# Exponentials by bits on VectorE: which engine writes the bits, when V's weights are loaded, and where the last branches stand

## The chip, the cores and the metric

The kernel runs on one core of one Trainium2 chip. A core has TensorE (matrix products, called PE in the profile; its weight loads PEld), VectorE (DVE), ScalarE (ACT), GpSimd (POOL) and SyncE (SP, which here issues nearly all DMAs). The metric is the time of one execution on the device in microseconds; lower is better. Inputs and output are bf16.

## The reference

Two branches work on the same input x of 2048 rows and 1024 columns, and a gate mixes them.

```
x = A_x
g = _sigmoid((x * gate_w).sum(-1, keepdims=True))
a = _A_ref(x, ...)          # complex linear recurrence over 2048 steps, 1024 states, then a projection and a skip
b = _B_ref(x, wqkv, wo)     # attention, 32 heads of width 32, softmax over all 2048 keys, then a projection
return g * a + (1 - g) * b
```

What matters for the change is the softmax of the attention: 32 x 2048 x 2048 exponentials of scaled scores.

## The kernel before, in words

The program has two versions of the computation. The fast one (class `FastPath`) leaves out what guards against odd numbers; at its end a flag tells whether any sum was out of range, and if so every engine branches into the slow and safe version. With the given inputs the fast one's result stands. Everything below is the fast one.

**Attention.** The 32 heads go in 8 groups of 4. A group has 8 query blocks of 256 rows (a "unit", U), and a unit has 8 bursts, each of 256 keys: 512 bursts in all. One burst is 8 score products on TensorE (`burst`, L1627: 4 heads x 2 blocks of 128 keys, 256 queries each) into two of three PSUM slots ("S"), and two exponentials on ScalarE of 128 x 1024 each (L1646). The exponentials, in bf16, are the weights of the products with V (`pv`, L1732), which add up over a unit in one PSUM bank ("O"). After a unit, VectorE takes the reciprocal of the sums and scales (`normalize`, L1745 and L1746).

**Exponentials on VectorE.** In 206 of the bursts, listed in pairs by `X_PLAN` and `X_AT`, the last 256 of the 2048 columns are not ScalarE's. VectorE multiplies and clips them out of PSUM into an int32 tile `xi` (L1636, "x_in"), and ScalarE's second exponential of that burst is then 128 x 768 (L1643). That instruction has the x_in of its burst as an explicit dependency. The high 16 bits of an element of `xi` are the whole part of a power of two, the low 16 bits the fraction. Two bursts make a batch (a pair), of 512 columns, 103 batches in all; `xi` has two buffers. `x_ops` turns a batch into bf16 bits: two steps on VectorE make a polynomial of the fraction in the f32 tile `xq` (L1670, L1671), a third on VectorE adds the scaled whole part (L1667), and a step on GpSimd scales, adds and writes the bits into `xp` (L1668). `xp` has one buffer. `x_pv` then issues four products per burst with V (L1711), as part of the sum in bank O.

When a unit has two batches, they come from its bursts 0 and 2 and its bursts 4 and 6. The first one's products stand in burst 7 of that unit, the second one's in burst 1 of the next.

**The rest.** The projections to Q, K and V of the next group (`d_qk` L1429, `d_v` L1448), the input side of the recurrence (`d_u` L1460), its output side (`d_c` L1507) and the last projection (`d_out` L1538) are "dense" chains. They all use one PSUM bank (7), one chain after the other, some four products after each burst. Each ends with an eviction on VectorE (L1436, L1454, L1464, L1520, L1550), and the next chain's first product waits for it. VectorE also runs the recurrence (L1356, L1365) up to about 720 us.

**What sets the order.** All of it is written out by one loop over the bursts (`build`), which plans with assumed durations: a time for VectorE (`dve_t`), a period of 1.83 us for each burst, and a place to put each VectorE operation. Each engine takes its instructions strictly in this order; `Sched` derives semaphore waits from tokens for tiles. A writer of a tile waits for its last readers. The planner knows nothing of the waits of a writer on readers.

**Loads and the end.** The weights of the next group's Q, K and V are loaded by SP at set bursts of the running group (`W_AT`; K's and V's at the group's first burst, `pg == 0`, L1074). At the end (`tail`), each of the last two row blocks gets two products (L2032), an eviction of one half on ScalarE and of the other on VectorE (L2041, L2045), and a store. Between the two blocks' products stands a product for the flag (L2035), and ahead of VectorE's two evictions the flag's copy (L2043). In `stream` each engine then waits for the flag, loads it into a register (L2103) and branches (L2104). SP, after its branch, waits for the last two stores.

```
i2, p2 = [("xi", b % 2, 0), ("xi", b % 2, 1)], [("xp", 0), ("xp", 1)]
self.dve(... scalar_tensor_tensor(xq[:], hi, 128.0 / X_K, xq[:], ALU.mult, ALU.add), i2 + ["xq"], ["xq"], "x_q")
self.pool(... tensor_scalar(bits, xq[:], X_K, 128.0 * (E0 + 126.0), ALU.mult, ALU.add), ["xq"], p2, "x_p")
```

Of the kernel before, what the change touches and what calls it, by code (L numbers as in the profile page):

```python
# [931 lines left out]
RING = 60  # L932
C_LOADS = 32
W_AT = (38, 0, 17)

X_AT = ((0, 2), (4, 6), (0, 4))
X_PLAN = (64, 72, 80, 84, 88, 92, 96, 100, 104, 108, 112, 116, 120, 124, 128, 132, 136, 144, 152, 156, 160, 164, 168, 172, 176, 180, 184, 188, 192, 200, 208, 216, 220, 224, 228, 232, 236, 240, 244, 248, 252, 256, 260, 264, 268, 272, 276, 280, 284, 288, 292, 296, 300, 304, 308, 312, 316, 320, 324, 328, 332, 336, 344, 348, 352, 356, 360, 364, 368, 372, 376, 380, 384, 388, 392, 396, 400, 404, 408, 412, 416, 420, 424, 428, 432, 436, 440, 444, 448, 452, 456, 460, 464, 468, 472, 476, 480, 484, 488, 492, 496, 500, 504)
# [8 lines left out]
RC_LATE = 0.25  # L946
X_A = SCALE * math.log2(math.e) * 65536.0
X_LO = -127.0 * 65536.0
E3, E2, E1, E0 = 0.0780245226404788, 0.2260671649, 0.6958335355, 0.9999252185627155
X_K = 128.0 * E3 / 65536.0 ** 3  # L950


# [10 lines left out]
class FastPath:  # L963

    def __init__(self, nc, S, es, d, flag):
# [28 lines left out]
        self.xi = T("xi", [128, 2, 2 * X_COLS], I32)  # L994
        self.xq = T("xq", [128, 2 * X_COLS], F32)
        self.xp = T("xp", [128, 2 * X_COLS], BF)
        self.ut = T("ut", [128, 2, 512], F32)
        self.ht = T("ht", [128, 2, 512], BF)
        self.prow = self.ht[0:40, 0, 0:128]
# [655 lines left out]

    def x_ops(self, b):

        xi, xq, xp = self.xi[:, b % 2], self.xq, self.xp
        lo = xi.bitcast(mybir.dt.uint16)[:, 0::2]
        hi = xi.bitcast(mybir.dt.int16)[:, 1::2]  # L1660
        bits = xp.bitcast(mybir.dt.int16)[:]
        w = 65536.0
        i2, p2 = [("xi", b % 2, 0), ("xi", b % 2, 1)], [("xp", 0), ("xp", 1)]

        def last():
            assert self.x_out == len(self.x_done)
            self.dve(lambda e: e.scalar_tensor_tensor(xq[:], hi, 128.0 / X_K, xq[:], ALU.mult, ALU.add), i2 + ["xq"], ["xq"], "x_q")  # L1667
            self.pool(lambda e: e.tensor_scalar(bits, xq[:], X_K, 128.0 * (E0 + 126.0), ALU.mult, ALU.add), ["xq"], p2, "x_p")  # L1668
            self.x_done.add(b)
        return [(0.61, DEP, lambda: self.dve(lambda e: e.scalar_tensor_tensor(xq[:], lo, E2 / E3 * w, lo, ALU.add, ALU.mult), i2, ["xq"], "x_q")),  # L1670
                (0.61, DEP, lambda: self.dve(lambda e: e.scalar_tensor_tensor(xq[:], xq[:], E1 / E3 * w * w, lo, ALU.add, ALU.mult), ["xq"] + i2, ["xq"], "x_q")),  # L1671
                (X_LAST, DEP, last)]
# [84 lines left out]
    def build(self):  # L1757
# [24 lines left out]
        for g in range(1, GROUPS):  # L1782
            for c in range(4):
                proj[g][c].after = W_AT[1] + 4
                proj[g][8 + c].after = max(16 * c, W_AT[0] + 4)
        proj[0] = [self.d_qk(0, 0, 2), self.d_qk(0, 0, 3)]
        us, cs = [], []
# [26 lines left out]
        for p in range(first, NBURST):  # L1814
# [43 lines left out]

            if pg == W_AT[1 if g else 2] and g + 1 < GROUPS:
                self.ld_w(g + 1, 1)  # L1860
                if g:
                    self.ld_w(g + 1, 2)
            if pg == W_AT[0] and g + 1 < GROUPS:
                assert not proj[0]
                self.ld_w(g + 1, 0)
# [119 lines left out]
    def tail(self):  # L1985

        S, ps, OT, wo, dve = self.S, self.ps, self.OT, self.wo, self.dve
        chk, rc, osum = self.chk, self.rc, self.osum
        z = self.ut[:, 1, 0:34]
        dve(lambda e: e.memset(z, 0.0), [], ["z"] + [("ut", 1)])  # L1990

        def check(u0, u1, s0, s1, c):

            ra = rc[:, u0:u1].rearrange("p u g -> p (u g)")
            t, z2 = self.ut[:, 0, 0:8 * (u1 - u0)], self.ut[:, 1, 128:128 + s1 - s0]
            rcs, oss = [("rc", u) for u in range(u0, u1)], [("os", u) for u in range(s0, s1)]
            dve(lambda e: e.tensor_scalar(t, ra, RC_MAX, None, ALU.is_le), rcs, [("ut", 0)])
            dve(lambda e: e.scalar_tensor_tensor(t, ra, RC_MIN, t, ALU.is_ge, ALU.mult, accum_out=chk[:, c:c + 1]), rcs + [("ut", 0)], [("ut", 0), ("chk", c)])
            dve(lambda e: e.scalar_tensor_tensor(z2, osum[:, s0:s1], 0.0, z[:, s0:s1], ALU.mult, ALU.is_equal, accum_out=chk[:, c + 1:c + 2]), oss + ["z"], ["z2", ("chk", c + 1)])

        def preload(r):
            for n in range(2):
                S.op("pe", lambda e, r=r, n=n: e.matmul(ps[:, 2 + r, :], self.ident[:], self.hilo[2 * r][n], start=(n == 0), stop=False),
                     reads=["ident", ("hi", 2 * r), ("lo", 2 * r)], name="preload", writes=[("tb", 2 + r)] + ([("S", 1)] if r == n == 0 else []), **({} if r == n == 0 else dict(acc=[("S", 1)])))
        assert self.os_n == 32 and not self.bg2
        check(0, 63, 0, 32, 0)
        self.pv(4 * NBURST - 8, 4 * NBURST - 4)
        preload(0)
        self.pv(4 * NBURST - 4, 4 * NBURST - 2)
        self.pv(4 * NBURST - 2, 4 * NBURST)  # L2010
        preload(1)
        ov = ps[:, 6, 0:264].rearrange("p (a c) -> p a c", a=8)
        On = self.On[:, 1]
        dve(lambda e: e.reciprocal(rc[:, 63], ov[:, :, 32]), ["O"], [("rc", 63)], "rcp")
        for t in range(2):
            o = On[:, t].rearrange("p (h c) -> p h c", h=4)
            dve(lambda e, t=t, o=o: e.scalar_tensor_tensor(o, ov[:, 4 * t:4 * t + 4, 0:32], self.gcol[:, 1, 14 + t:15 + t],
                                                           rc[:, 63, 4 * t:4 * t + 4].unsqueeze(2).to_broadcast([128, 4, 32]), ALU.mult, ALU.mult,
                                                           accum_out=osum[:, 32 + t:33 + t]), ["O", ("rc", 63), "g1"], [("On", 1, t), ("os", 32 + t)], "norm")
            S.op("pe", lambda e, t=t: e.matmul(ps[:, t, 0:128], On[:, t], self.ident[:], start=True, stop=True),  # L2020
                 reads=[("On", 1, t), "ident"], name="xp", **(dict(writes=[("S", 0), ("xp", t)]) if t == 0 else dict(acc=[("S", 0)], writes=[("xp", t)])))
        for t in range(2):
            self.act(lambda e, t=t: e.activation(OT[:, 7, 1792 + 128 * t:1920 + 128 * t], ps[:, t, 0:128], ACT.Copy), [("xp", t)], [("OT", 7, 7, t)], "xp")
        check(63, 64, 32, 34, 2)
        dve(lambda e: e.tensor_reduce(chk[:, 4:5], chk[:, 0:4], AX.X, ALU.add), [("chk", c) for c in range(4)], [("chk", 4)])
        dve(lambda e: e.tensor_scalar(self.badb[:, 0:1], chk[:, 4:5], 545.5, None, ALU.is_lt), [("chk", 4)], ["badb"])

        for r in range(2):
            for cb in range(2):
                bank = 2 + r + 2 * cb  # L2030
                w = dict(acc=[("tb", bank)]) if cb == 0 else dict(writes=[("tb", bank)] + ([("S", 2)] if r == 0 else []), **({} if r == 0 else dict(acc=[("S", 2)])))
                S.op("pe", lambda e, r=r, cb=cb, bank=bank: e.matmul(ps[:, bank, :], OT[:, 7, 1792 + 128 * r:1920 + 128 * r], wo[7][0][:, 512 * cb:512 * (cb + 1)],  # L2032
                                                                    start=(cb == 1), stop=True), reads=[("OT", 7, 7, r), "wo7"], name="tail", **w)
            if r == 0:
                S.op("pe", lambda e: e.matmul(ps[0:1, 7, 0:1], self.badb[:, 0:1], self.badb[:, 1:2], start=True, stop=True), reads=["badb", "one"],  # L2035
                     writes=[("bank", 7)], name="flag")
        for r in range(2):
            fb = self.fin_n % 8 // 2
            self.fin_n += 2
            o = self.fin[fb]  # L2040
            self.act(lambda e, o=o, r=r: e.activation(o[:, 0:512], ps[:, 2 + r, :], ACT.Copy), [("tb", 2 + r)], [("fin", fb, 0)], "evac_t")  # L2041
            if r == 0:
                self.flag_op = dve(lambda e: e.tensor_copy(self.flag[:], ps[0:1, 7, 0:1]), [("bank", 7)], ["flag"], "flag")  # L2043
                self.flag_op.force_signal = True
            dve(lambda e, o=o, r=r: e.scalar_tensor_tensor(o[:, 512:1024], ps[:, 4 + r, :], 1.0, self.sum7[2 * r + 1], ALU.mult, ALU.add),  # L2045
                [("tb", 4 + r), ("sum7", 2 * r + 1)], [("fin", fb, 1)], "evac_t")
            self.st_out(14 + r, fb)
def bass_gated_mix__ssm_conv_s5__mha_block__prompt_kernel(
    nc: bass.Bass,
    A_x: bass.AP,  # L2050
# [18 lines left out]
    with ExitStack() as es:  # L2069
# [20 lines left out]
        def stream(name, e):  # L2090
# [10 lines left out]
            e.wait_ge(sems[fast.flag_op.lane], fast.flag_op.tick)  # L2101
            with e.register("bad_" + name) as r:
                e.reg_load(r, flag[0:1, 0:1])  # L2103
                br = e.br_cmp(r, 0, on_true="done_" + name, on_false="bad_" + name, comp_op="IS_EQ")  # L2104
                br.branch_hint(loc[0])
                with e.bass.body("bad_" + name):
                    if name == "sp":
                        S.final_waits(e, sems, True)
                        e.nop().then_inc(go, 1)
                    e.wait_ge(go, 1)  # L2110
                    S2.emit(name, e, sems2)
# [1 line left out]
                        S2.final_waits(e, sems2)  # L2113
                    e.br("done_" + name)
                e.bass.switch_bb("done_" + name)
            if name == "sp":
                S.final_waits(e, sems, True)

        @block.sync
        def _(e):  # L2120
# [45 lines left out]
```

## Time and profile before

| | |
|---|---|
| median of 3 runs | 924.5 us (923.71 to 927.6) |
| the profiled execution | 923.76 us, its span 921.9 us |
| ScalarE busy | 903.8 us (98%) |
| TensorE busy | 882.3 us (96%) |
| VectorE busy | 769.6 us (83%) |
| GpSimd busy | 101.9 us (11%) |
| granted TensorE clock | 0.996 of full speed |

The span runs from the first to the last instruction of the program; the execution's time holds a little more at both ends. A row of the groups or of the timeline names line, engine, operation, the tiles written and read (out<-in), shapes and count. In the groups, "busy, mean ns" is followed by the engine's idle time just before and by what ended it. In the timeline the columns are the start and the duration in microseconds, and a bracket gives idle time before and what ended it. PSUM tiles are all called f_ps. Matmuls are pipelined and their ends are modelled. GpSimd's durations are rough.

### The profile page before, as it was taken

The numbers are of one execution on the slowest core, as the hardware profiler recorded it, in microseconds if no ns is written. First come the engines' busy times: TensorE is split into PE (matmuls) and PEld (weight loads), VectorE is DVE, ScalarE is ACT, GpSimd is POOL, SyncE is SP. The second block draws the span as 40 slices with busy tenths as digits, with TensorE's granted clock in tenths as the row PEclk, the third lists the DMA queues.
The fourth block names the chain that finished last, engine by engine and source line by source line (L and its number), as shares of the span: only waits on it lengthen the run. The fifth ranks groups of instructions, "written<-read, shape, count | busy, mean of one in ns | idle before, by whom it ended". The sixth has DMA issues, their size and how long they took to land.

```text
span 921.9 us, 33840 instructions
## 1 busy us (share of the span) xinstructions
PE 882.3 (96%) x15095; PEld 503.8 (55%) x15316; DVE 769.6 (83%) x1365; ACT 903.8 (98%) x1034; POOL 101.9 (11%) x167
## 2 busy tenths in 40 slices
PE   8899999999999999999999999999999999999996
PEld 4555744556555565556555565555655556545553
DVE  2788989999989999999999989999998655676765
ACT  6999999999999999999999999999999999999996
POOL 2000001102101111111111111011010010000010
PEclk9999999999999999999999999999999999999998
DMA  9549757630553202361022420612002014324312
GB/s 206 82 100 157 107 111 137 144 84 16 105 117 89 60 20 65 96 134 39 19 74 65 106 55 23 135 58 75 20 17 53 31 50 137 118 85 132 112 62 75
DMA packets 170983, 77.70 MB, mean 84 GB/s; under 512 B 147280, under 2 KB 155472, under 8 KB 170832
## 3 DMA queue, kind: packets, MB, share of 16 engines
q1 hardware_dynamic: 168672, 74.94, 35.6%
q8 instruction: 121, 1.98, 0.9%
q10 hardware_dynamic: 2160, 0.53, 0.3%
q14 instruction: 30, 0.25, 0.1%
HBM read 25.18 MB, written 20.97 MB: 50 GB/s over the span
## 4 chain that ended last, share of the span: by engine, by line
PE 53%; ACT 30%; DVE 13%; issue 2%; DMA 1%; POOL 0%; DVEq 0%; SPq 0%
ACT f_pt L1646 23%; PE f_ps L1732 12%; PE f_ps L1627 10%; PE f_ps L1507 8%; PE f_ps L1429 8%; PE f_ps L1460 6%; PE f_ps L1448 5%; ACT f_pt L1643 5%; DVE f_xi L1636 3%; DVE f_ht L1365 2%; ACT f_cT L1646 1%; DVE f_ub L1464 1%; DVE f_Ag L1520 1%; PE f_ps L1711 1%; DVE f_xq L1670 1%
## 5 line engine op out<-in xcount | busy, mean ns | idle before, releaser
L1646 ACT ACTIVATE f_pt<-f_ps 128x1024 bf16<-128x1024 f32 x738 | 711.9, 1082 | 3.2 <-PE f_ps L1627 3.0
L1732 PEld LDWEIGHTS f_ps<-f_V,f_pt 128*128 128x128 bf16 x7140 | 221.7, 96 | 94.7 <-issue 65.9
L1732 PE MATMUL f_ps<-f_V,f_pt 128*128 128x33 bf16 x7140 | 256.9, 178 | 0.1
L1627 PE MATMUL f_ps<-f_Q,f_K 32*128 32x256 bf16 x4096 | 203.4, 273 | 10.5 <-ACT f_pt L1646 2.8
L1643 ACT ACTIVATE f_pt<-f_ps 128x768 bf16<-128x768 f32 x206 | 183.0, 889 | 0.0
L1668 POOL TENSOR_SCALAR f_xp<-f_xq 128x512 int16<-128x512 f32 x103 | 82.8, 804 | 598.7 <-DVE f_xq L1667 423.8
L1627 PEld LDWEIGHTS f_ps<-f_Q,f_K 32*128 32x128 bf16 x4096 | 60.8, 92 | 144.5 <-ACT f_pt L1646 117.6
L1460 PE MATMUL f_ps<-f_xT,f_wb 128*128 128x512 bf16 x448 | 117.7, 379 | 9.0 <-DVE f_ub L1464 1.7
L1429 PE MATMUL f_ps<-f_xT,f_wb 128*128 128x512 bf16 x406 | 106.7, 379 | 4.1 <-issue 0.4
L1636 DVE TENSOR_SCALAR f_xi<-f_ps 128x256 int32<-128x256 f32 x206 | 86.8, 421 | 25.8 <-PE f_ps L1627 21.5
L1365 DVE TENSOR_TENSOR_SCAN f_ht<-f_pf,f_init,f_ut 128x512 bf16<-128x512 f32 x64 | 81.1, 1275 | 0.0
L1671 DVE SCALAR_TENSOR_TENSOR f_xq<-f_xq,f_xi 128x512 f32<-128x512 f32 x103 | 71.0, 689 | 2.5
L1670 DVE SCALAR_TENSOR_TENSOR f_xq<-f_xi 128x512 f32<-128x512 uint16 x103 | 70.7, 686 | 2.5 <-POOL f_xp L1668 0.7
L1667 DVE SCALAR_TENSOR_TENSOR f_xq<-f_xi,f_xq 128x512 f32<-128x512 int16 x103 | 70.8, 687 | 1.9
L1507 PE MATMUL f_ps<-f_cT,f_hp 128*128 128x512 bf16 x240 | 67.6, 379 | 2.5 <-DVE f_Ag L1520 0.5
L1460 PEld LDWEIGHTS f_ps<-f_xT,f_wb 128*128 128x128 bf16 x512 | 40.1, 96 | 41.5 <-issue 10.1
L1448 PE MATMUL f_ps<-f_wb,f_xT 128*128 128x128 bf16 x896 | 59.3, 219 | 0.0
L1429 PEld LDWEIGHTS f_ps<-f_xT,f_wb 128*128 128x128 bf16 x464 | 36.1, 96 | 35.3 <-issue 7.6
L1448 PEld LDWEIGHTS f_ps<-f_wb,f_xT 128*128 128x128 bf16 x896 | 50.4, 97 | 3.8 <-issue 3.8
L1464 DVE CAST f_ub<-f_ps 128x512 bf16<-128x512 f32 x64 | 44.0, 687 | 7.8 <-PE f_ps L1460 6.9
L1745 DVE RECIPROCAL f_rc<-f_ps 128x8 f32<-128x8 f32 x63 | 13.0, 206 | 40.5 <-PE f_ps L1711 36.2
L1356 DVE TENSOR_TENSOR f_ut<-f_ht,f_tq 128x512 f32<-128x512 bf16 x64 | 43.0, 691 | 0.6
(149 smaller groups left out, 818.1 us busy)
## 6 DMA issues: line engine op xcount, KB each, us to landing
u_scratch<-f_ub SPq DMA_DIRECT2D x64, 128.0 KB, 1.9
f_ub<-u_scratch SPq DMA_DIRECT2D x32, 256.0 KB, 2.8
ag_scratch<-f_Ag SPq DMA_DIRECT2D x32, 256.0 KB, 2.0
f_hp<-ag_scratch SPq DMA_DIRECT2D x32, 256.0 KB, 3.0
f_wb<-in_B_wqkv_dram SPq DMA_DIRECT2D x21, 256.0 KB, 3.9
out_dram<-f_xT SPq DMA_DIRECT2D x16, 256.0 KB, 2.0
f_cT<-in_B_wo_dram SPq DMA_DIRECT2D x5, 256.0 KB, 6.4
f_OT<-f_On SPq DMA_TRANSPOSE x63, 2.6
```

The source lines that it names most:

```text
L1365: ops.append((1.2, 0.0, lambda ri=ri: dve(lambda e: e.tensor_tensor_scan(ht[:, ri, :], rr, ut[:, ri, :], self.init[:, ri, j:j + 1], ALU.mu ...
L1429: mms.append((1, lambda e, f, l, a=a, w=w: e.matmul(ps[:, bank, :], w[:, a, :], xT[:, a, 512 * ch:512 * (ch + 1)], start=f, stop=l), [tok] ...
L1448: m = e.matmul(ps[:, bank, 128 * q:128 * (q + 1)], xT[:, a, 128 * kt:128 * (kt + 1)], w[:, a, :], start=(a == 0), stop=(a == 7))
L1460: mms.append((1, lambda e, f, l, a=a: e.matmul(ps[:, 7, :], bT[:, (2 * n + ri) % 3, a, :], xT[:, a, 512 * ch:512 * (ch + 1)], start=f, sto ...
L1507: mms.append((1, lambda e, f, l, j=j, ri=ri, h=h: e.matmul(ps[:, 7, :], h[:, cols], cT[ri][:, j, 512 * cb:512 * (cb + 1)], start=f, stop=l ...
L1627: m = e.matmul(ps[:, 2 * sl[h // 2] + h % 2, 256 * kl:256 * (kl + 1)], K[32 * h:32 * h + 32, g % 2, 128 * kt:128 * (kt + 1)], Q[32 * h:32 ...
L1636: first = self.dve(lambda e: e.tensor_scalar(self.xi[:, b % 2, X_COLS * n:X_COLS * (n + 1)], ps[:, 2 * s + 1, 512 - X_COLS:512], X_A, X_LO ...
L1643: self.S.op("act", lambda e: e.activation(flat(self.tile[p]), flat(ps[:, 2 * s:2 * s + 2, :]), ACT.Exp, scale=SCALE), reads=[("S", s)], wr ...
L1646: self.act(lambda e: e.activation(self.tile[p], ps[:, 2 * s:2 * s + 2, :], ACT.Exp, scale=SCALE), [("S", s)], [("pt", p)], "exp")
L1668: self.pool(lambda e: e.tensor_scalar(bits, xq[:], X_K, 128.0 * (E0 + 126.0), ALU.mult, ALU.add), ["xq"], p2, "x_p")
L1670: return [(0.61, DEP, lambda: self.dve(lambda e: e.scalar_tensor_tensor(xq[:], lo, E2 / E3 * w, lo, ALU.add, ALU.mult), i2, ["xq"], "x_q") ...
L1732: m = e.matmul(ps[:, 6, o:o + 33], self.tile[p][:, h2, 256 * kl + 128 * qt:256 * kl + 128 * (qt + 1)], V[:, g % 2, 2 * i + kl, h, :], star ...
```

## The change

Three things are changed.

1. In `x_ops`, a new GpSimd step, issued first, makes the exponent's part of the bits from the high halves of `xi` into a new int16 tile `xe` of two buffers. VectorE's first two steps stay. Its third step multiplies the polynomial, adds `xe` and writes the bits into `xp` itself. GpSimd's old last step goes. The polynomial's coefficients change so that the constant term is exactly 1.
2. V's weights of the next group are loaded at the group's burst 6 (`V_AT`) instead of burst 0, for all groups but the first and the last; the projections of V may not start before burst 10.
3. In `tail`, the flag's product comes behind all four last products and the flag's copy behind both evictions. In `stream`, every engine waits for the last two stores ahead of its branch, and not SP alone behind it.

```
-E3, E2, E1, E0 = 0.0780245226404788, 0.2260671649, 0.6958335355, 0.9999252185627155
+E3, E2, E1, E0 = 0.0770672403, 0.227644978, 0.695116631, 1.0
...
+        self.xe = T("xe", [128, 2, 2 * X_COLS], mybir.dt.int16)
...
-        xi, xq, xp = self.xi[:, b % 2], self.xq, self.xp
+        xi, xq, xe = self.xi[:, b % 2], self.xq, self.xe[:, b % 2]
...
-        bits = xp.bitcast(mybir.dt.int16)[:]
+        bits = self.xp.bitcast(mybir.dt.int16)[:]
...
-        i2, p2 = [("xi", b % 2, 0), ("xi", b % 2, 1)], [("xp", 0), ("xp", 1)]
+        i2, e2, p2 = [("xi", b % 2, 0), ("xi", b % 2, 1)], [("xe", b % 2)], [("xp", 0), ("xp", 1)]
+        self.pool(lambda e: e.tensor_scalar(xe, hi, 128.0, 128.0 * (E0 + 126.0), ALU.mult, ALU.add), i2, e2, "x_e")
...
-            self.dve(lambda e: e.scalar_tensor_tensor(xq[:], hi, 128.0 / X_K, xq[:], ALU.mult, ALU.add), i2 + ["xq"], ["xq"], "x_q")
-            self.pool(lambda e: e.tensor_scalar(bits, xq[:], X_K, 128.0 * (E0 + 126.0), ALU.mult, ALU.add), ["xq"], p2, "x_p")
+            self.dve(lambda e: e.scalar_tensor_tensor(bits, xq[:], X_K, xe, ALU.mult, ALU.add), e2 + ["xq"], p2, "x_q")
...
+                proj[g][4 + c].after = V_AT + 4 if g > 1 else 0
...
-                if g:
-                    self.ld_w(g + 1, 2)
+            if pg == V_AT and 0 < g < GROUPS - 1:
+                self.ld_w(g + 1, 2)
...
-            if r == 0:
-                S.op("pe", lambda e: e.matmul(ps[0:1, 7, 0:1], ...), reads=["badb", "one"], writes=[("bank", 7)], name="flag")
+        S.op("pe", lambda e: e.matmul(ps[0:1, 7, 0:1], ...), reads=["badb", "one"], writes=[("bank", 7)], name="flag")
...
-            if r == 0:
-                self.flag_op = dve(lambda e: e.tensor_copy(self.flag[:], ps[0:1, 7, 0:1]), [("bank", 7)], ["flag"], "flag")
...
+        self.flag_op = dve(lambda e: e.tensor_copy(self.flag[:], ps[0:1, 7, 0:1]), [("bank", 7)], ["flag"], "flag")
...
                 e.reg_load(r, flag[0:1, 0:1])
+                S.final_waits(e, sems, True)
                 br = e.br_cmp(r, 0, on_true="done_" + name, on_false="bad_" + name, comp_op="IS_EQ")
...
-            if name == "sp":
-                S.final_waits(e, sems, True)
```

More of the change, by code (lines that the diff above doesn't have):

```diff
@@ L934 @@
 W_AT = (38, 0, 17)
+V_AT = 6
 X_AT = ((0, 2), (4, 6), (0, 4))
@@ L2033, in tail @@
                                                                     start=(cb == 1), stop=True), reads=[("OT", 7, 7, r), "wo7"], name="tail", **w)
-            if r == 0:
-                S.op("pe", lambda e: e.matmul(ps[0:1, 7, 0:1], self.badb[:, 0:1], self.badb[:, 1:2], start=True, stop=True), reads=["badb", "one"],
-                     writes=[("bank", 7)], name="flag")
+        S.op("pe", lambda e: e.matmul(ps[0:1, 7, 0:1], self.badb[:, 0:1], self.badb[:, 1:2], start=True, stop=True), reads=["badb", "one"],
+             writes=[("bank", 7)], name="flag")
         for r in range(2):
@@ L2041, in tail @@
             self.act(lambda e, o=o, r=r: e.activation(o[:, 0:512], ps[:, 2 + r, :], ACT.Copy), [("tb", 2 + r)], [("fin", fb, 0)], "evac_t")
-            if r == 0:
-                self.flag_op = dve(lambda e: e.tensor_copy(self.flag[:], ps[0:1, 7, 0:1]), [("bank", 7)], ["flag"], "flag")
-                self.flag_op.force_signal = True
             dve(lambda e, o=o, r=r: e.scalar_tensor_tensor(o[:, 512:1024], ps[:, 4 + r, :], 1.0, self.sum7[2 * r + 1], ALU.mult, ALU.add),
@@ L2047, in tail @@
             self.st_out(14 + r, fb)
+        self.flag_op = dve(lambda e: e.tensor_copy(self.flag[:], ps[0:1, 7, 0:1]), [("bank", 7)], ["flag"], "flag")
+        self.flag_op.force_signal = True
 def bass_gated_mix__ssm_conv_s5__mha_block__prompt_kernel(
@@ L2115, in stream @@
                 e.bass.switch_bb("done_" + name)
-            if name == "sp":
-                S.final_waits(e, sems, True)
         @block.sync
```

## The prediction

> **What bounds the kernel now.** I read the page first (busy shares, slices, groups), then the list of waits, then the timeline of three places where a pair's bits are made, then the last microseconds.
>
> ```profile
> PE 882.3 (96%) x15095; PEld 503.8 (55%) x15316; DVE 769.6 (83%) x1365; ACT 903.8 (98%) x1034; POOL 101.9 (11%) x167
> DVE  2788989999989999999999989999998655676765
> ...
> L1646 ACT ACTIVATE f_pt<-f_ps 128x1024 bf16<-128x1024 f32 x738 | 711.9, 1082 | 3.2 <-PE f_ps L1627 3.0
> ...
> L1643 ACT ACTIVATE f_pt<-f_ps 128x768 bf16<-128x768 f32 x206 | 183.0, 889 | 0.0
> L1668 POOL TENSOR_SCALAR f_xp<-f_xq 128x512 int16<-128x512 f32 x103 | 82.8, 804 | 598.7 <-DVE f_xq L1667 423.8
> ```
>
> ScalarE is the bound: it is busy for 903.8 of 921.9 us, with exponentials back to back, so a delay of its next input that is longer than the lead this input has is lost for good. VectorE stands at 8 or 9 tenths in slices 3 to 31 and at 5 to 7 after. GpSimd is nearly idle; its x_p step (L1668) waits far more than it works.
>
> ```profile
> POOL f_xp L1668 <- PE f_ps L1711: 174.8, 38, 7.2
> PEld f_ps L1627 <- ACT f_pt L1646: 117.6, 302, 1.0
> ...
> PEld f_ps L1711 <- POOL f_xp L1668: 1.7, 3, 0.9
> ...
> PE f_ps L1711 <- POOL f_xp L1668: 1.4, 3, 0.8
> ```
>
> The first row is what the forecast hangs on. There is one tile of finished bits, xp, and in 38 of 103 pairs its writer waits until TensorE has read the previous pair's bits (L1711). Today that writer is GpSimd, where nobody queues behind it. In the changed kernel the writer is VectorE's third step, and everything that VectorE has to do queues behind it; the changed program gives 40 of its 103 third steps a wait on TensorE. The second row says that TensorE runs ahead of ScalarE by under 0.4 us a burst; the last two that today's detour through GpSimd holds TensorE up for only 3.1 us in the whole run.
>
> **Part 1, the step itself.** GpSimd's one step per pair goes from the end of the chain to its beginning, VectorE keeps three steps of one size (below: 0.69 us, whether it reads 32-bit or 16-bit input), so I price the new third step at the old one's time. What is new is the wait. One late place, of VectorE, TensorE, GpSimd and ScalarE:
>
> ```profile
> 827.92 0.69 DVE L1667 SCALAR_TENSOR_TENSOR f_xq<-f_xi,f_xq 128x512 f32<-128x512 int16 x1
> 828.72 0.75 DVE L1550 SCALAR_TENSOR_TENSOR f_xT<-f_ps,f_gcol,f_hp 128x512 bf16<-128x512 f32 x1
> 828.93 0.26 PE L1711 MATMUL f_ps<-f_V,f_xp 128*128 128x33 bf16 x4
> 829.34 0.62 POOL L1668 TENSOR_SCALAR f_xp<-f_xq 128x512 int16<-128x512 f32 x1 [6.70 <-PE f_ps L1711]
> 829.57 0.42 DVE L1636 TENSOR_SCALAR f_xi<-f_ps 128x256 int32<-128x256 f32 x1
> 830.50 0.93 ACT L1643 ACTIVATE f_pt<-f_ps 128x768 bf16<-128x768 f32 x1
> ...
> 831.61 0.21 DVE L1745 RECIPROCAL f_rc<-f_ps 128x8 f32<-128x8 f32 x1 [1.62 <-PE f_ps L1711]
> ```
>
> The previous bits are read out at 828.93 + 0.26 = 829.19. The third step may then start at 829.22 (the reciprocal's row shows VectorE 0.03 behind TensorE) instead of 827.92: 1.30 us late. Behind it stand the eviction of the projections' bank (L1550) and the next pair's input (L1636). The third step ends at 829.91, the eviction with its accumulator's read at about 830.75, the input at 831.2 instead of 829.99. ScalarE's shortened exponential (L1643) is made to wait for that input, and starts today at 830.50: it becomes 0.7 us late. The reciprocal's 1.62 us of idle time takes up VectorE's own lag, so the loss happens once in each such place and does not pile up.
>
> The same in the busy stretch, now along TensorE:
>
> ```profile
> 549.45 0.69 DVE L1667 SCALAR_TENSOR_TENSOR f_xq<-f_xi,f_xq 128x512 f32<-128x512 int16 x1
> ...
> 550.24 0.69 DVE L1454 CAST f_V<-f_ps 128x512 bf16<-128x512 f32 x1
> ...
> 550.44 0.26 PE L1711 MATMUL f_ps<-f_V,f_xp 128*128 128x33 bf16 x4
> ...
> 551.33 1.05 PE L1448 MATMUL f_ps<-f_wb,f_xT 128*128 128x128 bf16 x16
> ...
> 552.31 0.40 PE L1627 MATMUL f_ps<-f_Q,f_K 32*128 32x256 bf16 x8
> 552.64 0.27 PEld L1732 LDWEIGHTS f_ps<-f_V,f_pt 128*128 128x128 bf16 x8 [0.21 <-issue]
> ...
> 552.76 2.90 ACT L1646 ACTIVATE f_pt<-f_ps 128x1024 bf16<-128x1024 f32 x3
> ```
>
> Bits read at 550.70, third step 550.73 to 551.42, eviction to 552.1; the next projection needs that bank and starts at 552.1 instead of 551.33, the next scores (L1627) at 553.1 instead of 552.31, and ScalarE's exponential, which today starts 0.05 us after them, is 0.8 us late. A place with a shorter wait:
>
> ```profile
> 451.65 0.68 DVE L1667 SCALAR_TENSOR_TENSOR f_xq<-f_xi,f_xq 128x512 f32<-128x512 int16 x1
> ...
> 452.16 0.26 PE L1711 MATMUL f_ps<-f_V,f_xp 128*128 128x33 bf16 x4
> ...
> 452.85 0.41 DVE L1636 TENSOR_SCALAR f_xi<-f_ps 128x256 int32<-128x256 f32 x1
> ...
> 453.73 0.93 ACT L1643 ACTIVATE f_pt<-f_ps 128x768 bf16<-128x768 f32 x1
> ```
>
> Here everything moves by 452.42 + 0.03 - 451.65 = 0.80; the input ends at 454.06 instead of 453.26 and ScalarE is 0.35 late, along TensorE by the same reckoning as above about 0.5. Going through the 40 places like this I find 28 of the wide kind (about 0.72 us, the mean of the two shown, a little to the low side) and 12 of the narrow (0.5): 28 x 0.72 + 12 x 0.5 = 26 us. Ends: nothing, were all of it absorbed, and 40 x 1.30 = 52, were no lead left. I take 26, between them, because the leads (0.5 us before L1643, 0.55 before the projections) are read from the places themselves.
>
> **Part 1, two further terms.** TensorE's waits on GpSimd's step go: at most -3.1 us, at least 0; I take -1, since TensorE has a lead of its own. Then the new first step (x_e) runs while VectorE's first two steps run. What such an overlap costs is seen where today's step met a VectorE operation on two tiles:
>
> ```profile
> 293.17 0.68 DVE L1356 TENSOR_TENSOR f_tq<-f_ht,f_Et 128x1024 bf16<-128x1024 bf16 x1
> ...
> 293.38 0.95 POOL L1668 TENSOR_SCALAR f_xp<-f_xq 128x512 int16<-128x512 f32 x1
> ...
> 293.77 1.10 DVE L1356 TENSOR_TENSOR f_ut<-f_ht,f_Et 128x1024 bf16<-128x1024 bf16 x1
> ```
>
> The second of two like operations took 1.10 instead of 0.68 us, and GpSimd's 0.95 instead of 0.62: 0.42 us for VectorE. All 103 pairs will have it, up to 43 us of VectorE's time; what matters is what leaves VectorE. In the 40 waiting pairs it falls into the wait and costs nothing. In the others it uses the 0.4 to 0.6 us of lead that the rows above show. I take +4; ends 0 and 26 (63 pairs x 0.42). [...]
>
> **Part 2, V's weights.** The load moves past six bursts in SP's queue, one load of 256 KB as before.
>
> ```profile
> 690.98 1.19 SPq L1074 DMA_DIRECT2D f_wb<-in_B_wqkv_dram  x2
> L1448 PE MATMUL f_ps<-f_wb,f_xT x64: 216/219/229, 711.4 to 717.0; 128*128 128x128 bf16 x64
> DMA to landing us min/median/max: 3.1/3.9/5.3
> ```
>
> This is the tightest group: issued some 11 us later, at about 702.5, it lands by 708 and is used at 711.4. The order of the projections doesn't change. I take 0; the cover is these 3 us, and a load that lost them would cost up to 3 us in this one group, the next transposes and stores in SP's queue 0.6 us that nobody waits for.
>
> **Part 3, the ending.**
>
> ```profile
> q8 instruction: 121, 1.98, 0.9%
> ...
> 915.67 0.14 DVE L2043 CAST flag<-f_ps 1x1 int32<-1x1 f32 x1 [0.42 <-PE f_ps L2035]
> 915.74 1.27 DVE L2045 SCALAR_TENSOR_TENSOR f_xT<-f_ps,f_Et 128x512 bf16<-128x512 f32 x2
> ...
> L2104 POOLq COMPARE_BRANCH  x1: 65/65/65, 916.4 to 916.4; - x1
> L2069 POOLq DRAIN  x1: 126/126/126, 916.9 to 916.9; - x1
> DMA to landing us min/median/max: 2.0/2.0/4.4
> ```
>
> The last line is of the 16 output stores: 2.0 us is usual, 4.4 the last. That one shares the DMA engines with the instruction fetches that follow the branches (a packet of q8 is 1.98 MB / 121 = 16 KB and holds one engine for 0.009 x 16 x 921.9 / 121 = 1.1 us). With all branches behind the stores the last lands in about 2.0: -2.4. The flag's copy no longer stands before the evictions: -0.15. The branch then follows the landing; GpSimd's took 0.5 from the compare to the next instruction: +0.5. Sum -2; ends -2.5, and +1, if the branch has to fetch its target first. The Trainium skill ("Runtime: NRT & Kernel Launch", Instruction fetch mechanics) says that a taken branch out of the fetched window stalls for a fetch; by that the term would lie near its upper end, but the 0.5 us here show no such stall.
>
> **The sum.** Against the profiled execution's 923.8 us (0.7 below the median of three runs, 924.5): 923.8 + 26 - 1 + 4 + 0 - 2 = 951 us.
>
> **Rivals.**
> *VectorE runs out of idle time.* In the first 70% it has little:
>
> ```profile
> 160.00:700.00 540.00, 527.48 (x9086) 302.85 (x9220) 499.60 (x844) 538.26 (x619) 72.82 (x108) 1.00 0.31 71
> ```
>
> 540 - 499.6 = 40 us idle (the third busy column), against 25 waits of about 1.0 and 72 overlaps of 0.42, 55 us. If the excess of 15 comes on top, 966. For it: the stretch's 9s; against: the run's own lengthening gives idle time back, and a late VectorE waits less.
> *The waits stay off the path.* The change then leaves -1 to -3 and -2: 920. It decides where ScalarE's lead over its input exceeds 1.2 us; the rows show 0.5. This is the case on the other side.
> *Half of it.* If TensorE and ScalarE have leads that the rows don't show (L1643's start is set by the exponential before it, which may itself move), 13 instead of 26: 938.
>
> **How the numbers follow.** The sum as it stands 0.54 (own range 942 to 960), VectorE out of idle time 0.25 (960 to 978), half 0.11, off the path 0.10. The range 936 to 970 leaves out the last and the upper part of the second, some 2 in 10. A measurement here can't tell less than about 0.5%, 4.6 us, from no change (the three runs span 3.9). Off the path gives -0.4%: 0.07 the same, 0.03 faster. Slower: 0.90.
>
> **What would show it.** In the profile after: a wait of VectorE's third step on L1711 of about 40 us in some 40 places; idle time of ScalarE before L1643 on VectorE's L1636, which is nil today; TensorE waiting on VectorE's evictions; fewer microseconds idle before the reciprocal; some of the first or second steps at 1.1 instead of 0.69; the last store landing in about 2 us. I am wrong if the third step waits and ScalarE's idle time does not grow, or if L1643 still starts without a wait.

## The result, and the profile after

| | before | after |
|---|---|---|
| median | 924.5 us (923.71 to 927.6) | 962.41 us (961.8 to 962.94) |
| ratio, 95% interval | | 1.041 (1.0399 to 1.0421) |
| the profiled execution, its span | 923.76, 921.9 us | 961.92, 960.2 us |
| ScalarE busy, idle | 903.8, 18.1 us | 915.9, 44.3 us |
| granted TensorE clock | 0.996 | 0.997 |

The changed kernel is 4.1% slower. The forecast was 951 us with a range of 936 to 970. The direction and the mechanism hold, and the size is 11 us short. The measured time also lies outside the 942 to 960 us that the prediction gave its own sum. Lines after the change are two or three higher: x_in is L1638, the two exponentials L1645 and L1648, the scores L1629, the products with the bits L1713, VectorE's three steps L1672, L1673 and L1670, GpSimd's new step L1666.

The page of the changed kernel, busy shares and groups (the last columns are busy time, mean ns of one, idle time before and what ended it):

```profile
PE 878.1 (91%) x15095; PEld 509.5 (53%) x15316; DVE 794.8 (83%) x1365; ACT 915.9 (95%) x1034; POOL 135.3 (14%) x167
...
L1648 ACT ACTIVATE f_pt<-f_ps 128x1024 bf16<-128x1024 f32 x738 | 703.3, 1045 | 18.1 <-PE f_ps L1629 16.5
...
L1666 POOL TENSOR_SCALAR f_xe<-f_xi 128x512 int16<-128x512 int16 x103 | 115.6, 1122 | 630.1 <-DVE f_xi L1638 630.1
L1645 ACT ACTIVATE f_pt<-f_ps 128x768 bf16<-128x768 f32 x206 | 172.5, 837 | 13.1 <-DVE f_xi L1638 12.8
...
L1670 DVE SCALAR_TENSOR_TENSOR f_xp<-f_xq,f_xe 128x512 int16<-128x512 f32 x103 | 70.8, 688 | 36.2 <-PE f_ps L1713 31.7
L1673 DVE SCALAR_TENSOR_TENSOR f_xq<-f_xq,f_xi 128x512 f32<-128x512 f32 x103 | 85.7, 832 | 2.5
L1672 DVE SCALAR_TENSOR_TENSOR f_xq<-f_xi 128x512 f32<-128x512 uint16 x103 | 85.2, 827 | 1.8
```

Its list of waits (microseconds in total, times, longest):

```profile
DVE f_rc L1747 <- PE f_ps L1713: 31.8, 37, 1.6
DVE f_xp L1670 <- PE f_ps L1713: 31.7, 37, 1.1
...
ACT f_pt L1648 <- PE f_ps L1629: 16.5, 55, 0.6
ACT f_pt L1645 <- DVE f_xi L1638: 12.8, 38, 0.5
PE f_ps L1509 <- DVE f_Ag L1522: 11.5, 14, 1.0
...
PE f_ps L1540 <- DVE f_xT L1552: 8.5, 13, 1.0
```

The new wait is there: VectorE's third step sits idle for TensorE's reading of the old bits in 37 places, 31.7 us. ScalarE has two kinds of idle time that it did not have. It waits 16.5 us for scores (3.0 before), and 12.8 us in front of the shortened exponential for x_in (nil before). TensorE waits for VectorE's evictions, 11.5 and 8.5 us in the rows shown. The span grew by 38.3 us, and ScalarE's idle time by 26.2 of them. The other 12.1 appear as busy time, though no work was added: exponentials in a row overlap a little in the record (in the prediction's late place before, one started at 830.50 while the three ahead of it, from 827.77 for 2.95, ended at 830.72), and each gap takes that overlap away as well. A single exponential without it is recorded as shorter (1045 ns in the mean instead of 1082), but the lost overlap is the larger part.

### The profile page after: what moved, and what is told of

It reads as the page before. It is cut to its first block, busy times and chain, and to the rows that moved or that the text cites. A ratio compares the mean times of both kernels' runs of the same rounds, so it can differ in the third digit from the quotient of the medians.

```text
span 960.2 us, 33832 instructions
## 1 busy us (share of the span) xinstructions
PE 878.1 (91%) x15095; PEld 509.5 (53%) x15316; DVE 794.8 (83%) x1365; ACT 915.9 (95%) x1034; POOL 135.3 (14%) x167
## 4 chain that ended last, share of the span: by engine, by line
PE 57%; DVE 27%; ACT 8%; issue 4%; SPq 1%; DMA 1%; POOL 1%; DVEq 0%
PE f_ps L1734 12%; PE f_ps L1629 10%; PE f_ps L1509 9%; PE f_ps L1431 8%; PE f_ps L1462 7%; ACT f_pt L1648 6%; PE f_ps L1540 5%; PE f_ps L1450 4%; DVE f_ht L1367 4%; DVE f_xp L1670 3%; DVE f_xi L1638 3%; DVE f_xq L1672 2%; DVE f_ub L1466 2%; DVE f_Ag L1522 2%; DVE f_tq L1358 2%
## 5 line engine op out<-in xcount | busy, mean ns | idle before, releaser
L1648 ACT ACTIVATE f_pt<-f_ps 128x1024 bf16<-128x1024 f32 x738 | 703.3, 1045 | 18.1 <-PE f_ps L1629 16.5
L1629 PE MATMUL f_ps<-f_Q,f_K 32*128 32x256 bf16 x4096 | 203.5, 273 | 8.4 <-ACT f_pt L1648 2.6
L1666 POOL TENSOR_SCALAR f_xe<-f_xi 128x512 int16<-128x512 int16 x103 | 115.6, 1122 | 630.1 <-DVE f_xi L1638 630.1
L1645 ACT ACTIVATE f_pt<-f_ps 128x768 bf16<-128x768 f32 x206 | 172.5, 837 | 13.1 <-DVE f_xi L1638 12.8
L1629 PEld LDWEIGHTS f_ps<-f_Q,f_K 32*128 32x128 bf16 x4096 | 60.7, 92 | 137.9 <-ACT f_pt L1648 95.3
L1431 PE MATMUL f_ps<-f_xT,f_wb 128*128 128x512 bf16 x406 | 106.8, 379 | 16.5 <-DVE f_Q L1438 5.6
L1638 DVE TENSOR_SCALAR f_xi<-f_ps 128x256 int32<-128x256 f32 x206 | 86.2, 418 | 20.4 <-PE f_ps L1629 18.8
L1670 DVE SCALAR_TENSOR_TENSOR f_xp<-f_xq,f_xe 128x512 int16<-128x512 f32 x103 | 70.8, 688 | 36.2 <-PE f_ps L1713 31.7
L1673 DVE SCALAR_TENSOR_TENSOR f_xq<-f_xq,f_xi 128x512 f32<-128x512 f32 x103 | 85.7, 832 | 2.5
L1672 DVE SCALAR_TENSOR_TENSOR f_xq<-f_xi 128x512 f32<-128x512 uint16 x103 | 85.2, 827 | 1.8
L1540 PE MATMUL f_ps<-f_cT,f_OT 128*128 128x512 bf16 x122 | 37.3, 380 | 11.4 <-DVE f_xT L1552 8.5
```

Of the source, the lines that this page charges most:

```text
L1431: mms.append((1, lambda e, f, l, a=a, w=w: e.matmul(ps[:, bank, :], w[:, a, :], xT[:, a, 512 * ch:512 * (ch + 1)], start=f, stop=l), [tok] ...
L1629: m = e.matmul(ps[:, 2 * sl[h // 2] + h % 2, 256 * kl:256 * (kl + 1)], K[32 * h:32 * h + 32, g % 2, 128 * kt:128 * (kt + 1)], Q[32 * h:32 ...
L1638: first = self.dve(lambda e: e.tensor_scalar(self.xi[:, b % 2, X_COLS * n:X_COLS * (n + 1)], ps[:, 2 * s + 1, 512 - X_COLS:512], X_A, X_LO ...
L1645: self.S.op("act", lambda e: e.activation(flat(self.tile[p]), flat(ps[:, 2 * s:2 * s + 2, :]), ACT.Exp, scale=SCALE), reads=[("S", s)], wr ...
L1648: self.act(lambda e: e.activation(self.tile[p], ps[:, 2 * s:2 * s + 2, :], ACT.Exp, scale=SCALE), [("S", s)], [("pt", p)], "exp")
L1666: self.pool(lambda e: e.tensor_scalar(xe, hi, 128.0, 128.0 * (E0 + 126.0), ALU.mult, ALU.add), i2, e2, "x_e")
```

## The experiments

Every kernel computes the whole result. The ratios are to the kernel before on the same chip. In the expectations W is the theory that the wait of the third step costs the time, and L that it is the lengthening of VectorE's steps by GpSimd's.

### The wait alone

The kernel before, whose third step still writes `xq` and leaves the bits to GpSimd, but now must wait until `xp` is read out:

```
-... xq[:], ALU.mult, ALU.add), i2 + ["xq"], ["xq"], "x_q")
+... xq[:], ALU.mult, ALU.add), i2 + ["xq"], ["xq"] + p2, "x_q")
```

> The kernel before, with only the wait added: VectorE's third step (which still writes xq) also waits until TensorE has read the previous pair's bits; GpSimd's last step stays behind it. Theory W: 40 places of 0.95 to 1.0 us, 960 to 964 us. Theory L: the wait alone gives the 26 us that the prediction had for it, about 950 us.

Measured: 959.5 us against 924.85, ratio 1.0372 (1.0353 to 1.0391), +34.7 us. Its waits:

```profile
DVE f_xq L1667 <- PE f_ps L1711: 46.3, 39, 2.3
...
ACT f_pt L1646 <- PE f_ps L1627: 17.1, 47, 1.2
ACT f_pt L1643 <- DVE f_xi L1636: 11.8, 38, 0.6
```

No step was moved to another engine, nothing was added, and yet nine tenths of the loss are here, with ScalarE's same two kinds of idle time. One wait written into an instruction list is nine tenths of the change's price; theory L's 950 is out, and W's 960 to 964 is missed by 0.5. The wait is longer here than in the changed kernel, 46.3 us in 39 places against 31.7 in 37: VectorE, whose first two steps are not lengthened here, arrives at the wait sooner.

### Two buffers of finished bits

The changed kernel with `xp` doubled, so that the third step has nothing to wait for:

```
-        self.xp = T("xp", [128, 2 * X_COLS], BF)
+        self.xp2 = T("xp", [128, 2, 2 * X_COLS], BF)
...
-        bits = self.xp.bitcast(mybir.dt.int16)[:]
+        bits = self.xp2.bitcast(mybir.dt.int16)[:, b % 2]
```

(The readers and the tokens take `b % 2` in the same way.)

> The changed kernel, with two buffers of finished bits (xp) in place of one: VectorE's third step then waits for nobody, everything else stays. Theory W (the wait for the previous bits is nearly the whole loss of 38 us): the 37 waits on TensorE go, ScalarE's idle time before its shortened exponentials goes, and the time is that of before less the ending's 2 us and up to 1 us of GpSimd's old detour: 921 to 923 us. Theory L (a good part, 10 us or more, is GpSimd's new first step lengthening VectorE's first two steps, which stays here): 931 to 937 us. If neither holds and the loss comes from the loads or the ending, it stays near 962 us.

Measured: 932.37 us, ratio 1.0082 (1.0068 to 1.0096). Its groups:

```profile
L1646 ACT ACTIVATE f_pt<-f_ps 128x768 bf16<-128x768 f32 x206 | 176.8, 858 | 0.0
...
L1671 DVE SCALAR_TENSOR_TENSOR f_xp<-f_xq,f_xe 128x512 int16<-128x512 f32 x103 | 70.6, 686 | 5.7
```

The wait on TensorE is gone, ScalarE's wait for x_in is gone, and 30.0 of the 37.9 us with them. With parts 2 and 3, which this kernel still has, worth -1.8 (last experiment), 932.37 - 924.85 + 1.8 = 9.3 us are left for GpSimd's new step. Theory W's 921 to 923 us is missed, and L's 931 to 937 holds.

### The third step behind the next pair's input

The other way to take the queue away from the waiting step: one buffer as in the changed kernel, but where the previous pair's products stand in the same burst, VectorE's third step is issued behind the x_in of the next burst.

```
+            third = lambda: self.dve(... bits, xq[:], X_K, xe, ... e2 + ["xq"], p2, "x_q")
+            if self.x_out_p == self.p:
+                self.x_put.append(third)
+            else:
+                third()
...
             second = self.burst(p)
+            while self.x_put:
+                self.x_put.pop(0)()
```

> The changed kernel, still with one buffer of bits, but wherever the previous pair's products stand in the same burst, VectorE's third step is issued behind the next burst's x_in instead of ahead of the eviction and that x_in. By then TensorE has read the previous bits, and the step waits for nobody. Theory Q (the loss is what queues behind the waiting step, the eviction and the x_in, and not the late bits): the same as with two buffers, 930 to 934 us, no wait of the third step on TensorE. Theory B (the bits themselves come too late for their products): 940 us or more, and TensorE waits for VectorE ahead of L1713's products.

Measured: 933.81 us, ratio 1.0095 (1.0079 to 1.011). No wait of the third step on TensorE is left, though the bits are made later than in the changed kernel:

```profile
L1645 ACT ACTIVATE f_pt<-f_ps 128x768 bf16<-128x768 f32 x206 | 177.9, 864 | 0.3 <-DVE f_xi L1638 0.2
...
L1670 DVE SCALAR_TENSOR_TENSOR f_xp<-f_xq,f_xe 128x512 int16<-128x512 f32 x103 | 70.4, 683 | 2.7
```

So it is not late bits that cost time but what queues behind the waiting step: without a second buffer and with the bits later still, the time is within 1.5 us of the kernel with two buffers (theory Q).

### GpSimd's new step alone

The kernel before, with the new GpSimd step added in every pair and its result read by nobody (extra work; the bits are made as before):

```
+        xe = self.xe[:, b % 2]
+        self.pool(lambda e: e.tensor_scalar(xe, hi, 128.0, 128.0 * 127.0, ALU.mult, ALU.add), i2, [("xe", b % 2)], "x_e")
```

> The kernel before, plus GpSimd's new first step on every pair with a result that nobody reads. VectorE's first and second steps will show about 0.14 us more in the mean (0.83 in place of 0.69), as in the changed kernel. Theory W: that stays inside the leads, 924 to 928 us. Theory L: 934 us or more.

Measured: 938.34 us, ratio 1.0148 (1.013 to 1.0166), +13.5 us. Theory W, that the lengthening stays inside the leads, is out. Its groups show VectorE's first two steps lengthened just as in the changed kernel:

```profile
L1675 DVE SCALAR_TENSOR_TENSOR f_xq<-f_xq,f_xi 128x512 f32<-128x512 f32 x103 | 85.6, 831 | 2.5
L1674 DVE SCALAR_TENSOR_TENSOR f_xq<-f_xi 128x512 f32<-128x512 uint16 x103 | 84.8, 824 | 3.0 <-POOL f_xp L1672 1.2
```

### The same, writing without reading

The kernel before, with a GpSimd memset of `xe` in the same place, waiting for the same x_in, its result read by nobody:

```
+        self.pool(lambda e: e.memset(xe, 16256), i2, [("xe", b % 2)], "x_e")
```

> The kernel before, plus a GpSimd step in the place of the new first step that waits for the same x_in and writes the same tile, but reads none (a memset; nobody reads its result). With the reading step the time rose by 13.5 us to 938. Theory P (VectorE's operations on two tiles and GpSimd's reads shut each other out): VectorE's first two steps return to 0.69 us in the mean and the time to 924 to 926 us. Theory G (any work of GpSimd beside VectorE costs, or the additional semaphore traffic): 934 to 940 us.

Measured: 924.83 us against 924.69, ratio 1.0003 (0.9993 to 1.0012). Its groups:

```profile
L1667 POOL MEMSET f_xe<- 128x512 int16 x103 | 56.3, 547 | 307.0 <-DVE f_xi L1637 307.0
...
L1675 DVE SCALAR_TENSOR_TENSOR f_xq<-f_xq,f_xi 128x512 f32<-128x512 f32 x103 | 71.1, 690 | 2.5
L1674 DVE SCALAR_TENSOR_TENSOR f_xq<-f_xi 128x512 f32<-128x512 uint16 x103 | 70.7, 686 | 2.5 <-POOL f_xp L1672 0.7
```

VectorE's steps are back at 0.69 us and nothing is lost, with as many instructions and semaphores on GpSimd. Theory P holds: it is GpSimd's reading beside VectorE's reading of two operands that costs. The two added operations differ in length too (0.55 against 1.12 us in the mean; the reading one takes 0.62 at its shortest). The Trainium skill ("SBUF — State Buffer", Who interferes with whom) states the same split: a VectorE instruction with two SBUF inputs contends with a GpSimd instruction that reads SBUF, not with one that only writes it. These two runs agree: 0.82 and 0.83 us a step in the one, 0.69 in the other. How long the one blocks the other in this case, the runs show: 0.28 us are added to a pair in the changed kernel, since 827 + 832 - 686 - 689 = 284 ns.

### V's load, the ending, and both

Three kernels: the kernel before with V's load later (`V_AT`, part 2 of the diff), with the ending (part 3), and with both.

```
+            if pg == V_AT and 0 < g < GROUPS - 1:
+                self.ld_w(g + 1, 2)
```

> The kernel before with part 2 alone (V's weights at burst 6 instead of burst 0). The prediction's reading is that nothing waits for this load, so 924 to 925 us and a ratio whose interval holds 1. The rival reading, from parts 2 and 3 together at 0.9978 and part 3 alone at 0.9988, is that the later load is worth about 0.9 us: 0.999, with K's weights landing sooner behind the group's first burst.

> The kernel before with part 3 alone (flag's product and copy last, all branches behind the last stores). V's load worth nothing: the same as parts 2 and 3 together, 922.5 to 923.5 us, ratio 0.998. If V's later load gives part of the 1.8 us, this one is nearer to before, 924 us or more.

> The kernel before with parts 2 and 3 of the change alone (V's weights at burst 6, the branches behind the last stores). All theories: V's load is worth nothing, the last store lands in 2.1 in place of 4.4 us, and the branch costs 0.5 us behind it: 2 us faster than before, 922 to 923 us. If moving V's load frees something at the groups' beginnings it is below 922.

| | median us | before, same chip | ratio (95%) |
|---|---|---|---|
| V's load later | 924.14 | 925.69 | 0.9985 (0.9976 to 0.9994) |
| the ending | 923.92 | 924.69 | 0.9988 (0.9977 to 0.9998) |
| both | 923.06 | 924.85 | 0.9978 (0.997 to 0.9987) |

Parts 2 and 3 together are worth -1.8 us, and the kernel that has only these has the lowest median of all that ran. V's load alone has an interval that leaves out 1, so the reading that nothing waits for it is not borne out; the ending alone gains less than both, as its second expectation had it.

V's load shows itself in one place, SP's queue at 131 us. Before, and with the load later (start, duration):

```profile
131.06 1.20 SPq L1074 DMA_DIRECT2D f_wb<-in_B_wqkv_dram  x2
...
134.29 0.49 SPq L1477 DMA_DIRECT2D f_ub<-u_scratch  x1
```

```profile
131.74 0.58 SPq L1075 DMA_DIRECT2D f_wb<-in_B_wqkv_dram  x1
...
134.13 0.50 SPq L1478 DMA_DIRECT2D f_ub<-u_scratch  x1
```

The read of `u_scratch`, issued behind the loads in that queue, is what VectorE's next operation waits for. In the lists of waits of the two kernels VectorE waits 1.1 and 0.5 us for it:

```profile
DVE f_ht L1356 <- DMA f_ub<-u_scratch: 1.1, 1, 1.1
```

```profile
DVE f_ht L1357 <- DMA f_ub<-u_scratch: 0.5, 1, 0.5
```

This wait is 1.1 to 1.6 us in all five kernels with the load at burst 0 and 0.4 to 0.7 in all five with the later one. That it is what the later load gains isn't shown: in these two profiles the operation starts at 138.04 and 138.06 us, since the kernel with the later load was already 0.67 us behind there (VectorE's eviction ahead of it starts at 136.56 against 135.89).

The ending differs between kernels. First the changed kernel: the output stores' landing (min, median, max), VectorE's branch and its next instruction (durations in ns, start in us). Then the same of the kernel with parts 2 and 3 alone.

```profile
DMA to landing us min/median/max: 2.0/2.1/2.5
...
L2106 DVEq COMPARE_BRANCH  x1: 84/84/84, 959.3 to 959.3; - x1
...
L2070 DVEq DRAIN  x1: 54/54/54, 959.9 to 959.9; - x1
```

```profile
DMA to landing us min/median/max: 2.0/2.0/3.1
...
L2105 DVEq COMPARE_BRANCH  x1: 84/84/84, 919.3 to 919.3; - x1
...
L2069 DVEq DRAIN  x1: 53/53/53, 921.1 to 921.1; - x1
```

In both the last stores land sooner than the 4.4 us of before (the 3.1 is an earlier store; the last two have a median of 2.1). In the changed kernel VectorE goes from its branch to the next instruction in 0.6 us, in the other in 1.8. From the last reciprocal of the units to the end of the span it is 21.26 us before, 19.34 in the changed kernel and 20.70 with parts 2 and 3 alone: a gain of 1.9 or of 0.6. The kernels fall into two kinds: all three with part 1 and the new ending branch in 0.6 us and need 19.2 to 19.5 from that reciprocal, both with the new ending alone branch in 1.8 or 1.9 and need 20.6 or 20.7. The five with the old ending need 20.7 to 21.6, so the gain of 0.6 is no larger than their scatter. The source of the branch is the same in both kinds; only the code ahead of it differs. The Trainium skill ("Runtime: NRT & Kernel Launch", Instruction fetch mechanics) says that a taken branch stalls for a fetch when its target lies outside the window already fetched. The 1.8 us would fit that: between 919.3 and 921.1 us the one trace has four packets of instructions, between 959.3 and 959.9 the other has none. But no run moved the code by itself, and the trace does not say which engine a packet is for, so this remains an explanation by argument.

## Why the prediction was right, and where it was short

**The bound and the wait: right.** The forecast had about 40 us of waiting in some 40 places; it is 31.7 in 37, the idle time before the third step, of all causes, being 36.2. The signs it named are all there: ScalarE idle before the shortened exponential on x_in, TensorE waiting on evictions, less idle time before the reciprocal (31.8 us against 36.2), first and second steps up to 1.1 us, the last store in about 2 us. That the waits sum to 31.7 us and not 40 fits the lengthened first two steps, behind which the third arrives later (46.3 us where they are not lengthened). The rivals that the waits stay off the path (920) and that half of them do (938) are gone: the wait alone costs 34.7 us.

**The term "28 x 0.72 + 12 x 0.5 = 26": mis-sized, 34.7 alone.** Taken out of the changed kernel instead of added to the one before, the wait is worth 30.0 us; by either, 26 was too little. What was wrong is the lead that the prediction gave TensorE. A narrow place shows it best, the one that the prediction took at 451.65. Before, and then the changed kernel:

```profile
451.00 2.95 ACT L1646 ACTIVATE f_pt<-f_ps 128x1024 bf16<-128x1024 f32 x3
...
452.25 0.68 DVE L1436 CAST f_Q<-f_ps 128x512 bf16<-128x512 f32 x1
...
453.02 0.55 PEld L1429 LDWEIGHTS f_ps<-f_xT,f_wb 128*128 128x128 bf16 x4
...
453.26 0.81 PE L1429 MATMUL f_ps<-f_xT,f_wb 128*128 128x512 bf16 x3
...
454.00 0.40 PE L1627 MATMUL f_ps<-f_Q,f_K 32*128 32x256 bf16 x8
...
454.45 1.12 ACT L1646 ACTIVATE f_pt<-f_ps 128x1024 bf16<-128x1024 f32 x1
```

```profile
463.12 2.89 ACT L1648 ACTIVATE f_pt<-f_ps 128x1024 bf16<-128x1024 f32 x3
...
464.61 0.69 DVE L1670 SCALAR_TENSOR_TENSOR f_xp<-f_xq,f_xe 128x512 int16<-128x512 f32 x1 [0.45 <-PE f_ps L1713]
...
465.22 0.68 DVE L1438 CAST f_Q<-f_ps 128x512 bf16<-128x512 f32 x1
...
465.96 0.55 PEld L1431 LDWEIGHTS f_ps<-f_xT,f_wb 128*128 128x128 bf16 x4 [0.81 <-DVE f_Q L1438]
...
466.19 0.81 PE L1431 MATMUL f_ps<-f_xT,f_wb 128*128 128x512 bf16 x3 [0.94 <-DVE f_Q L1438]
466.27 0.81 ACT L1645 ACTIVATE f_pt<-f_ps 128x768 bf16<-128x768 f32 x1 [0.26 <-DVE f_xi L1638]
...
466.94 0.40 PE L1629 MATMUL f_ps<-f_Q,f_K 32*128 32x256 bf16 x8
...
467.38 1.02 ACT L1648 ACTIVATE f_pt<-f_ps 128x1024 bf16<-128x1024 f32 x1 [0.30 <-PE f_ps L1629]
```

Measured from the start of the three exponentials (the first row of each), the eviction starts 0.85 us later than before (2.10 against 1.25), the projections 0.81 (3.07 against 2.26), the scores 0.82 (3.82 against 3.00), the next full exponential 0.81 (4.26 against 3.45). Nothing on TensorE absorbs anything here. The prediction's 0.5 is what is left of its 0.80 when the 0.33 between the eviction's end (452.93) and the first product's start (453.26) counts as lead. But the product has a weight load in front of it. In the changed kernel that load starts 0.06 behind the eviction's end (465.90), and the product 0.23 behind the load. Before, the load started at 453.02, 0.09 behind the eviction: the true lead was 0.03 us. The shortened exponential, 0.42 us late (466.27 against 453.73 from the prediction's row), was priced well at 0.35, but it is not the link that ends last.

The wide places of the late kind have the same error. The one that the prediction took at 827.92, before and after:

```profile
827.77 2.95 ACT L1646 ACTIVATE f_pt<-f_ps 128x1024 bf16<-128x1024 f32 x3
...
829.79 0.34 PEld L1538 LDWEIGHTS f_ps<-f_cT,f_OT 128*128 128x128 bf16 x3
...
830.77 0.40 PE L1627 MATMUL f_ps<-f_Q,f_K 32*128 32x256 bf16 x8
...
831.22 2.03 ACT L1646 ACTIVATE f_pt<-f_ps 128x1024 bf16<-128x1024 f32 x2
```

```profile
862.17 2.89 ACT L1648 ACTIVATE f_pt<-f_ps 128x1024 bf16<-128x1024 f32 x3
...
865.08 0.33 PEld L1540 LDWEIGHTS f_ps<-f_cT,f_OT 128*128 128x128 bf16 x3 [0.88 <-DVE f_xT L1552]
...
866.05 0.40 PE L1629 MATMUL f_ps<-f_Q,f_K 32*128 32x256 bf16 x8
...
866.50 2.86 ACT L1648 ACTIVATE f_pt<-f_ps 128x1024 bf16<-128x1024 f32 x3 [0.29 <-PE f_ps L1629]
```

From the same start the first weight load is 0.89 us later (2.91 against 2.02), the scores and the exponential 0.88 (3.88 against 3.00, 4.33 against 3.45). Here the prediction priced the link through x_in, 0.7, and left TensorE's out, because 0.55 us between the eviction's end and the first product looked like a cover. In the busy stretch, where it did follow TensorE, it had 0.8, and the profile after shows 0.87 (from the start of the three exponentials to the next full one 4.37 us against 3.50). With 0.88 and 0.81 in place of 0.72 and 0.5 the prediction's own count of places gives 28 x 0.88 + 12 x 0.81 = 34 us; the wait alone measured 34.7. That TensorE's link, and not x_in's, ends last is read from these rows; no run cut one of the two without the other.

**The steps' overlap, "+4; ends 0 and 26": right beside the wait.** Wait and new step together cost 962.41 - 924.5 + 1.8 = 39.7 us, so the new step beside the wait costs 39.7 - 34.7 = 5.0. Alone it costs 13.5: much of a lengthened step falls into the wait that follows, as the prediction had it, and the wait is shorter beside it. In the narrow place above, the third step starts 0.84 us late (1.49 against 0.65 from the exponentials' start), of which only 0.45 is waiting. The split depends on the order: with the wait taken away, the same step costs 9.3, more than twice the prediction's 4. The 39.7 takes parts 2 and 3 at the -1.8 that they have by themselves; the changed kernel's ending gains 1.3 us more than that, and then wait and step are worth so much more. A pair's lengthening is 0.28 us and not 0.42. TensorE's relief from the old step (-1) is inside these 5.0 and was not measured apart. Its bound of 3.1 counts twice: the 1.7 and the 1.4 us stand before weight loads and products of the same three places (at 441, 497 and 539 us), so 1.7 was the most it could be.

**VectorE out of idle time: true in part.** With the wait removed, the new step's cost arises where that rival said. From the reciprocals of the units, the kernel with two buffers falls behind the kernel before by 9.7 us up to the one that stands at 706 us before (0.6 of it ahead of the first), and by 0.8 us in all after it; with the new step alone it is 13.5 (0.3 of it ahead of the first) and 0.45. The rival's time of 966 needed the wait and this excess to add, and they do not: added alone they cost 34.7 and 13.5, together 39.7. That it is VectorE's idle time that runs out is not shown by a run. Still it is the share given to this rival that took the stated range up to 970: the prediction's own sum ended at 960, and the measured 962.4 came about by a larger wait and not by this rival. That the range held is in part luck.

**V's load, "0": that nobody waits for SP's queue failed in one place.** VectorE waited there 1.1 us, and 0.5 or 0.6 with the load later. Part 2 alone is worth 0.6 to 2.2 us by its interval, part of which that one wait could explain.

**The ending, "-2": right for this kernel.** From the last reciprocal it is 19.34 instead of 21.26 us, -1.9, with the last store at 2.0 to 2.5 us instead of 4.4. With the same edits in the kernel before it is -0.6, with VectorE's branch at 1.8 us; the end of +1 that the prediction kept for a branch that fetches its target was the right thing to keep.

So the 11.6 us between the forecast's sum (950.8) and the median of 962.4 are, by this split, 8.7 of the wait (34.7 against 26), 2.0 of the new step (5.0 against +4 - 1), 0.2 of load and ending, and 0.7 of the base (924.5 against 923.8). The terms add up because the 5.0 is a difference; the measured ones are the wait alone, the step alone and parts 2 and 3 together.

## What to carry to other kernels

Before a step moves to a busier engine, list the waits that its old place takes for it, and look at what will queue behind each of them: the wait for one buffer stood in 38 places on GpSimd, 174.8 us in all, where the old step held TensorE up for 1.7 us at most, and the same wait alone on VectorE cost 34.7 us; a second buffer, or issuing the step behind what others need, takes nearly all of it back. A lead is counted to the first instruction of the chain that waits, weight load included, and not to the first product. An idle engine is not free either: a step that reads SBUF beside VectorE's steps on two operands cost 13.5 us by itself, one that only writes cost none.

## What the runs showed that was not expected

- A weight load stands 0.23 us ahead of the first product of a 512-wide chain (465.96 and 466.19) and starts 0.06 us after the eviction that it waits for; in the profile of before the two looked like 0.33 us of lead.
- The same branch of VectorE took 0.6 us to its next instruction in three kernels and 1.8 or 1.9 in two others whose ending is the same and whose code ahead of it differs.
- GpSimd's step on 128 x 512 lasts 1.12 us in the mean beside VectorE's steps (L1666) and 0.62 at the least; the old one's median was 0.62.
- ScalarE's loss shows by a third as busy time: 12.1 of 38.3 us come from lost overlap between exponentials in a row.
